# First expert of the second token chunk: where its weight blocks are loaded, summed and split

## The chip, the cores and the metric

One core of a Trainium2 chip. The metric is the device time of one execution in microseconds (us), as the median of the runs. TensorE (PE) multiplies, VectorE (DVE), ScalarE (ACT) and GpSimd (POOL) work beside it, and SyncE (SP) issues nearly all DMA transfers. Each engine works through its own queue in order; semaphores tie the queues together.

## The reference

Rotary attention over 2 batches, 8 heads, 576 positions and head width 64, and then a mixture of four experts on all 1152 tokens of width 512:

```python
out = 0
for e in range(4):
    h = np.maximum(x @ w1[e], 0.0)          # 1152x512 by 512x1024
    out += p[:, e:e + 1] * (h @ w2[e])      # 1152x1024 by 1024x512
```

`x` is the attention output, `p` the normalised domain probabilities. All is float32.

## The kernel before, in words

A float32 operand is held as two float32r parts, high and low, and a product is made of three matmuls (high by high, high by low, low by high). A weight block is 512 KB: two of the eight 128-wide slices of the hidden axis. `Weights.load` brings a block into a raw buffer (`wr`, on SP's queue), and `Weights.split` makes its parts: ScalarE copies the high part (`wh`), and then GpSimd subtracts (`wl`). There are NRAW = 2 raw buffers in the pool `wpool` and a ring of NRING = 5 pairs of split parts. `Weights.next` is one load and one split.

The tokens are done in two chunks: 512 tokens (chunk 0, woven into the attention of the second batch), and then the other 640 (chunk 1, class `Moe1`). In chunk 1 the first layer is done by seven products instead of eight block products: the tokens are cut in two halves of 320, the weight block in four quarters a11, a12, a21, a22, and p1 to p7 are products of sums of token blocks (t1 to t4, class `Quarters`) by quarters or by four sums of quarters (s0 to s3). `Weights.sum` makes those four sums of a block in a buffer `sf` (four instructions of 128x256, line 516), and splits them like a block: `sh` on ScalarE, `sl` on GpSimd. A product is six matmuls of 128x320 (lines 737 to 739). What it leaves in a PSUM bank is worked off by VectorE (adds, line 767, and the low part hL of the hidden values, line 777) and by ScalarE (a copy of p1, line 744, and the high part hH with the relu, line 775). The eight PSUM banks go round: a product takes the bank of the product eight places before it, and waits until that one has been worked off. The second layer (lines 816 to 818) is 120 matmuls of 128x512 for an expert, into five banks `po`; at its end VectorE mixes each bank into `acc` by the probabilities (lines 609 and 611), and the mix of the last expert of a chunk is followed by the DMA of the result (line 617).

Nothing reorders the work here: the order on each engine is that in which the code emits it. Chunk 1's first expert has another order than the rest. Its w1 blocks (key 0) come already split from chunk 0's last steps; then its four w1 blocks are loaded once more for the sums alone (key 2), and then the four w2 blocks (key 1). All p1, then all p2 are done first, and then p6, p7, p5, p4, p3 block by block. In what follows S1 to S4 are the blocks for the sums, W1 to W4 the w2 blocks ("weight blocks 3, 4" of the second layer are W3 and W4), and block 1 to 4 the rounds of the five products. In names as `wr_0_2_1` and `sh_1`, blocks are counted from 0. S3 and S4 have two raw buffers of their own in the pool `sums`, which takes the room that the attention leaves; all other blocks share the two of `wpool`. A load waits until its buffer's last reader is done. The calls of `load`, `split` and `next` between the products in `first_layer` and at the end of the kernel function decide where all this stands.

Of the kernel before, what the change touches and what calls it, by code (L numbers as in the profile page):

```python
# [55 lines left out]
def kernel(  # L56
# [17 lines left out]
    nc = tc.nc  # L74
# [57 lines left out]
    def split(eng_h, eng_l, src, hi, lo):  # L132

        if eng_h is nc.scalar:
            nc.scalar.activation(out=hi, in_=src, func=AF.Copy)  # L135
        elif eng_h is nc.gpsimd:
            nc.gpsimd.tensor_scalar(
                out=hi, in0=src, scalar1=1.0, scalar2=1.0, op0=ALU.mult, op1=ALU.mult
            )
        else:  # L140
            nc.vector.tensor_copy(hi, src)
        eng_l.tensor_tensor(out=lo, in0=src, in1=f32(hi), op=ALU.subtract)  # L142


    class Pair:
# [9 lines left out]
        def load(self, s, queue=nc.sync, heads=((0, 2),)):  # L155

            hp, nm = self.hp, self.nm
            src = {"k": k, "q": q, "v": v}[s]
            x = self.pool.tile([P, 2, NS, D], F32, tag=f"raw{s}", name=f"raw{s}{nm}")
            hs = src[self.b, 2 * hp : 2 * hp + 2]  # L160
            for i, (a, z) in enumerate(heads):
                queue.dma_start(
                    out=x[:, a:z, 0:NR, :], in_=hs[a:z, 0:SM, :].rearrange("h (p r) d -> p h r d", r=NR)
                )
                if i:
                    continue
                for j in range(2):
                    rows = slice(j * ST, (j + 1) * ST)
                    if s == "v":
                        queue.dma_start(out=x[rows, :, NR, :], in_=hs[:, SM:S, :].rearrange("h p d -> p h d"))  # L170
                    else:
                        queue.dma_start(out=x[rows, 0, NR, :], in_=hs[j, SM:S, :])
            self.raw[s] = x
# [285 lines left out]
    class Weights:  # L459
# [14 lines left out]
        def load(self):  # L474
            if self.loaded == len(self.order):
                return
            key = self.order[self.loaded]
            c, e, which, fb = key
            lo, hi = fb * FB * P, (fb + 1) * FB * P
            src, f = (w2[e, lo:hi, :], DM) if which == 1 else (w1[e, :, lo:hi], FB * P)  # L480
            late = which == 2 and fb >= NRAW
            raw = (self.pool if late else wpool).tile(
                [P, FB * DM], F32, tag="raw", name="wr%d_%d_%d_%d" % key, bufs=NRAW
            )
            nc.sync.dma_start(
                out=raw.rearrange("p (a f) -> p a f", f=f), in_=src.rearrange("(a p) f -> p a f", p=P)
            )
            self.raw[key] = raw, f
            self.loaded += 1
# [17 lines left out]
        def sum(self, raw, e, fb):  # L507

            a = raw.rearrange("p (j k h f) -> p j k h f", j=2, h=2, f=P)
            a11, a12, a21, a22 = (a[:, j, :, h, :] for h in range(2) for j in range(2))  # L510
            x = self.pool.tile([P, 4, 2, P], F32, tag="sf", name=f"sf{e}_{fb}", bufs=2)
            for o, p, q, op in (
                (0, a21, a22, ALU.add), (2, a11, a21, ALU.subtract), (1, x[:, 0], a11, ALU.subtract),
                (3, a12, x[:, 1], ALU.subtract),
            ):
                nc.vector.tensor_tensor(out=x[:, o], in0=p, in1=q, op=op)  # L516
            sh, sl = (
                self.pool.tile([P, 4, 2, P], F32R, tag=f"s{t}", name=f"s{t}{e}_{fb}", bufs=NF // FB) for t in "hl"
            )
            split(nc.scalar, nc.gpsimd, x, sh, sl)  # L520
            self.sums[e, fb] = sh, sl
# [177 lines left out]
    class Moe1(Moe):  # L699
# [3 lines left out]
            p1=("a11", "x00"), p2=("a12", "x10"), p3=("s3", "x11"), p4=("a22", "t4"), p5=("s0", "t1"),  # L703
# [78 lines left out]
        def first_layer(self, e):  # L782

            nb = NF // FB
            self.hh = {}
            if e == 0:
                for p in ("p1", "p2"):
                    for i in range(nb):
                        self.product(e, i, p)
                wts.split()  # L790
            for i in range(nb):
                for p in ("p6", "p7", "p5", "p4", "p3") if e == 0 else ("p1", "p6", "p7", "p5", "p2", "p4", "p3"):
                    self.product(e, i, p)
                    if p == "p4" and (e or i):
                        wts.next()
                if e == 0 and i == 0:
                    wts.split()
                elif e == 0 and i in (1, 2):
                    wts.next()
            for f in self.lows:  # L800
                f()
            self.lows = []
# [56 lines left out]
    NE, NRAW, NRING = 3, 2, 5  # L859
    wts = Weights()  # L860
# [201 lines left out]
    with ExitStack() as chunk1:  # L1062
        wts.pool = chunk1.enter_context(tc.tile_pool(name="sums", bufs=1, side="right", reuse_waits="tile"))
        wts.load()
        wts.load()
        wts.split()
        for x in moe0[0].mixes:
            moe0[0].mix(*x)
        chunk0.close()
        wts.load()  # L1070
        wts.split()
        moe = Moe1(chunk1, quarters[0])
        for e in range(E):
            moe.expert(e)
# [43 lines left out]
```

## Time and profile before

| | us |
|---|---|
| median of 3 runs | 579.5 (579.2 to 581.85) |
| span of the profiled execution | 577.8 |
| TensorE busy | 548.1 (95%) |
| VectorE busy | 333.6 (58%) |
| ScalarE busy | 278.9 (48%) |
| GpSimd busy | 334.1 (58%) |

The profile gives the profiled execution's time as its span, from the first to the last instruction; the median of the runs is 1.7 us above that. TensorE is the busiest engine, so the first question is when it stands still, and what ended each of these idle times. The second is at which clock it ran, which the profile gives as the granted share of full speed for any stretch. Attention and chunk 0 end at about 356.7 us from the span's start; first expert, first layer: 356.7 to 384.0; its second layer: 384.0 to 417.4; the other three experts: from 417.4 on.

### The profile page before, as it was taken

To read this page: it belongs to the slowest core of one execution; us is meant where nothing else is said; L and a number is where in the kernel's file an instruction comes from. 1 tells how busy PE (TensorE), PEld (TensorE's weight loads), DVE (VectorE), ACT (ScalarE), POOL (GpSimd) and SP (SyncE) were. 2 spreads that over 40 slices of the span, in tenths; PEclk is the share of its full clock that TensorE was granted. 3 is DMA by queue.
4 is the path that set the end of the run, shared out by engine and by line. 5 is a ranking of instruction groups with operands and counts; after the bars stand their busy time and mean duration, and the time that the engine had idled before them with its cause. 6 is when DMAs were issued, how large, how long until landed. Compare 5 with 4: busy or idle time off the path is not lost.

```text
span 577.8 us, 8600 instructions
## 1 busy us (share of the span) xinstructions
PE 548.1 (95%) x3229; PEld 479.6 (83%) x3229; DVE 333.6 (58%) x590; ACT 278.9 (48%) x545; POOL 334.1 (58%) x228
## 2 busy tenths in 40 slices
PE   4898998999999999999999989879999999999996
PEld 3788877888888888888888878868899899889985
DVE  5588898244363435344245446875777687677702
ACT  5688887555444544554446543453244234324300
POOL 7999964458614972386443493465664674465300
PEclk9999999999999999999999999998999999999999
DMA  5235112252234123422232223423232223223002
GB/s 150 72 112 141 21 45 96 71 175 96 84 100 137 57 71 97 135 75 74 78 97 74 73 67 124 138 74 109 74 110 73 74 79 105 74 73 110 2 0 91
DMA packets 42459, 50.67 MB, mean 88 GB/s; under 512 B 7218, under 2 KB 32050, under 8 KB 42418
## 3 DMA queue, kind: packets, MB, share of 16 engines
q1 hardware_dynamic: 41618, 49.38, 27.9%
q10 hardware_dynamic: 800, 0.75, 0.5%
q8 instruction: 25, 0.41, 0.3%
q14 instruction: 16, 0.13, 0.1%
HBM read 43.34 MB, written 2.36 MB: 79 GB/s over the span
## 4 chain that ended last, share of the span: by engine, by line
PE 74%; DVE 8%; ACT 7%; POOL 5%; issue 2%; DMA 2%; SPq 0%; ACTq 0%; POOLq 0%; DVEq 0%
PE po L816 6%; PE po L817 6%; PE po L818 6%; PE sc L282 5%; PE ph L601 4%; PE ph L603 4%; PE ph L602 4%; PE p L737 4%; PE p L738 4%; PE p L739 4%; PE po L578 4%; PE po L576 4%; PE po L577 4%; PE pp L315 4%; ACT e L301 3%; PE x L417 2%
## 5 line engine op out<-in xcount | busy, mean ns | idle before, releaser
L142 POOL TENSOR_TENSOR wl<-wr,wh 128x1024 fp32r<-128x1024 f32 x64 | 154.9, 2424 | 138.8 <-ACT wh L135 138.8
L135 ACT ACTIVATE wh<-wr 128x1024 fp32r<-128x1024 f32 x64 | 67.4, 1053 | 38.5 <-PE po L578 16.6
L293 DVE TENSOR_REDUCE mx<-sc 128x1 f32<-128x576 f32 x72 | 54.1, 752 | 37.9 <-PE sc L282 37.4
L142 POOL TENSOR_TENSOR sl<-sf,sh 128x1024 fp32r<-128x1024 f32 x16 | 38.4, 2401 | 50.9 <-ACT sh L135 50.9
L816 PE MATMUL po<-wh,hH 128*128 128x512 f32 x160 | 63.6, 398 | 3.1 <-DVE hL L777 3.1
L301 ACT ACTIVATE e<-sc,mx 128x576 f32<-128x576 f32 x72 | 53.3, 740 | 21.8 <-DVE mx L293 21.4
L817 PE MATMUL po<-wl,hH 128*128 128x512 f32 x160 | 63.4, 396 | 0.0
L818 PE MATMUL po<-wh,hL 128*128 128x512 f32 x160 | 63.3, 395 | 0.0
L562 DVE SCALAR_TENSOR_TENSOR hL<-ph,hH 128x512 fp32r<-128x512 f32 x32 | 22.1, 691 | 61.0 <-ACT hH L561 61.0
L576 PE MATMUL po<-wh,hH 128*128 128x512 f32 x128 | 52.3, 409 | 0.0
L601 PE MATMUL ph<-xH,wh 128*128 128x512 f32 x128 | 51.5, 402 | 0.0
L315 PE MATMUL pp<-ident,e 128*128 128x128 f32 x288 | 45.4, 282 | 5.5 <-DVE e L387 3.2
L516 DVE TENSOR_TENSOR sf<-wr 128x256 f32<-128x256 f32 x32 | 40.2, 1294 | 17.8 <-DMA wr<-in_moe_w_dram 17.8
L578 PE MATMUL po<-wh,hL 128*128 128x512 f32 x128 | 50.3, 393 | 0.0
L332 ACT ACTIVATE ptH<-pp 128x512 fp32r<-128x512 f32 x64 | 38.1, 595 | 25.1 <-PE x L365 17.3
L603 PE MATMUL ph<-xH,wl 128*128 128x512 f32 x128 | 50.1, 392 | 0.0
L336 DVE TENSOR_TENSOR ptL<-pp,ptH 128x512 fp32r<-128x512 f32 x64 | 43.9, 685 | 10.8 <-ACT ptH L332 10.3
L602 PE MATMUL ph<-xL,wh 128*128 128x512 f32 x128 | 50.1, 391 | 0.0
L577 PE MATMUL po<-wl,hH 128*128 128x512 f32 x128 | 50.0, 391 | 0.0
L775 ACT ACTIVATE hH<-p 128x320 fp32r<-128x320 f32 x64 | 27.4, 436 | 42.6 <-DVE p L767 42.2
L135 ACT ACTIVATE sh<-sf 128x1024 fp32r<-128x1024 f32 x16 | 17.0, 1061 | 61.9 <-DVE sf L516 61.9
L315 PEld LDWEIGHTS pp<-ident,e 128*128 128x128 f32 x288 | 34.5, 144 | 11.8 <-issue 2.0
(161 smaller groups left out, 1370.0 us busy)
## 6 DMA issues: line engine op xcount, KB each, us to landing
wr<-in_moe_w_dram SPq DMA_DIRECT2D x68, 512.0 KB, 3.5
k2T<-kT SPq DMA_DIRECT2D x14, 288.0 KB, 4.0
rawv<-in_v_dram SPq DMA_DIRECT2D x8, 256.0 KB, 2.9
out_dram<-acc SPq DMA_DIRECT2D x8, 256.0 KB, 2.6
rawk<-in_k_dram SPq DMA_DIRECT2D x7, 256.0 KB, 4.3
rawq<-in_q_dram SPq DMA_DIRECT2D x7, 256.0 KB, 3.0
rawv<-in_v_dram SPq DMA_DIRECT2D x16, 32.0 KB, 2.9
tabs<-in_rope_dram ACTq DMA_DIRECT2D x1, 320.0 KB, 3.5
```

The lines of the kernel that those rows point to most:

```text
L135: nc.scalar.activation(out=hi, in_=src, func=AF.Copy)
L142: eng_l.tensor_tensor(out=lo, in0=src, in1=f32(hi), op=ALU.subtract)
L315: nc.tensor.transpose(pp[:, c * P : (c + 1) * P], self.e[u][:, c * P : (c + 1) * P], ident)
L576: nc.tensor.matmul(po[t], lhsT=sH, rhs=wH, start=(f == 0), stop=False)
L577: nc.tensor.matmul(po[t], lhsT=sH, rhs=wL, start=False, stop=False)
L578: nc.tensor.matmul(po[t], lhsT=sL, rhs=wH, start=False, stop=(f == NF - 1))
L601: nc.tensor.matmul(o, lhsT=wH[:, kt], rhs=xh, start=(kt == 0), stop=False)
L602: nc.tensor.matmul(o, lhsT=wH[:, kt], rhs=xl, start=False, stop=False)
L603: nc.tensor.matmul(o, lhsT=wL[:, kt], rhs=xh, start=False, stop=(kt == KT1 - 1))
L816: nc.tensor.matmul(po[t], lhsT=sH, rhs=wH, start=(f == 0), stop=False)
L817: nc.tensor.matmul(po[t], lhsT=sH, rhs=wL, start=False, stop=False)
L818: nc.tensor.matmul(po[t], lhsT=sL, rhs=wH, start=False, stop=(f == NF - 1))
```

## The change

Four things are changed, all in chunk 1's first expert. W3 and W4 are loaded into the raw buffers of S3 and S4 (`late`). The load of W1 is emitted before chunk 0's last four mixes, the one of W2 after the p1 products, those of W3 and W4 after the p2 products. The four sums of S1 are made on GpSimd instead of VectorE. And the splits stand behind whole rounds of products: S2 between p1 and p2, S3 behind p2, S4 behind block 1, W1 behind block 2, W2 and W3 behind block 3, W4 behind block 4. With that the loads and splits of the following experts stand one call later than before.

```diff
-            late = which == 2 and fb >= NRAW
+            late = c and not e and which and fb >= NRAW
...
-                nc.vector.tensor_tensor(out=x[:, o], in0=p, in1=q, op=op)
+                (nc.vector if e or fb else nc.gpsimd).tensor_tensor(out=x[:, o], in0=p, in1=q, op=op)
...
             if e == 0:
-                for p in ("p1", "p2"):
-                    for i in range(nb):
-                        self.product(e, i, p)
+                for i in range(nb):
+                    self.product(e, i, "p1")
+                wts.next()
+                for i in range(nb):
+                    self.product(e, i, "p2")
+                wts.load()
                 wts.split()
+                wts.load()
             for i in range(nb):
                 for p in ("p6", "p7", "p5", "p4", "p3") if e == 0 else ("p1", "p6", "p7", "p5", "p2", "p4", "p3"):
                     self.product(e, i, p)
-                    if p == "p4" and (e or i):
+                    if p == "p4" and e:
                         wts.next()
-                if e == 0 and i == 0:
+                if e == 0:
                     wts.split()
-                elif e == 0 and i in (1, 2):
-                    wts.next()
+                    if i == 2:
+                        wts.split()
+                    elif i < 2:
+                        wts.load()
...
         wts.load()
         wts.load()
+        wts.load()
         wts.split()
         for x in moe0[0].mixes:
             moe0[0].mix(*x)
         chunk0.close()
-        wts.load()
-        wts.split()
         moe = Moe1(chunk1, quarters[0])
```

SyncE's queue at the end of chunk 0, before (`wr_0_2_n` are S3 and S4, `wr_0_1_n` W1 to W4, `wr_1_0_n` the next expert's first blocks, `acc` the results of chunk 0):

```order
L485 DMA wr_0_2_2_3960<-in_moe_w_dram 128x4x256
L485 DMA wr_0_2_3_3962<-in_moe_w_dram 128x4x256
L617 DMA out_dram<-acc_0_1510 128x512
L617 DMA out_dram<-acc_1_1511 128x512
L617 DMA out_dram<-acc_2_1512 128x512
L617 DMA out_dram<-acc_3_1513 128x512
L485 DMA wr_0_1_0_3983<-in_moe_w_dram 128x2x512
L485 DMA wr_0_1_1_4198<-in_moe_w_dram 128x2x512
L485 DMA wr_0_1_2_4214<-in_moe_w_dram 128x2x512
```

and in the changed kernel:

```order
L485 DMA wr_0_2_2_3960<-in_moe_w_dram 128x4x256
L485 DMA wr_0_2_3_3962<-in_moe_w_dram 128x4x256
L485 DMA wr_0_1_0_3964<-in_moe_w_dram 128x2x512
L617 DMA out_dram<-acc_0_1510 128x512
L617 DMA out_dram<-acc_1_1511 128x512
L617 DMA out_dram<-acc_2_1512 128x512
L617 DMA out_dram<-acc_3_1513 128x512
L485 DMA wr_0_1_1_4036<-in_moe_w_dram 128x2x512
L485 DMA wr_0_1_2_4090<-in_moe_w_dram 128x2x512
```

Only W1's load changes its place in the queue; what W3's and W4's loads wait for is changed by their buffers.

ScalarE's queue at the start of chunk 1, before (`sh_0` and `sh_1` are the high parts of the first two blocks' sums, the four rows of L744 the copies of p1, `hH` the hidden values of p2):

```order
L135 ACTIVATE sh_0_3969<-sf_0_3964 128x1024
L135 ACTIVATE sh_1_3990<-sf_1_3985 128x1024
L744 ACTIVATE p_0_0_4016<-p_0_4009 128x320
L744 ACTIVATE p_0_1_4025<-p_1_4018 128x320
L744 ACTIVATE p_0_2_4034<-p_2_4027 128x320
L744 ACTIVATE p_0_3_4043<-p_3_4036 128x320
L775 ACTIVATE hH_0_0_4051<-p_0_4005 128x320
```

and in the changed kernel:

```order
L135 ACTIVATE sh_0_3971<-sf_0_3966 128x1024
L744 ACTIVATE p_0_0_4007<-p_0_4000 128x320
L744 ACTIVATE p_0_1_4016<-p_1_4009 128x320
L744 ACTIVATE p_0_2_4025<-p_2_4018 128x320
L744 ACTIVATE p_0_3_4034<-p_3_4027 128x320
L135 ACTIVATE sh_1_4043<-sf_1_4038 128x1024
L775 ACTIVATE hH_0_0_4053<-p_0_3996 128x320
```

The second block's sums stand behind the four copies now.

ScalarE's queue from block 3 of the first layer on, before (`wh_0_1_1` to `wh_0_1_3` are W2 to W4; `hH_0_5` and `hH_0_4` belong to block 3, `hH_0_7` to block 4):

```order
L135 ACTIVATE wh_0_1_1_4216<-wr_0_1_1_4198 128x1024
L775 ACTIVATE hH_0_5_4247<-p_2_4239 128x320
L775 ACTIVATE hH_0_5_4247<-p_2_4251 128x320
L135 ACTIVATE wh_0_1_2_4263<-wr_0_1_2_4214 128x1024
L775 ACTIVATE hH_0_4_4072<-p_2_4267 128x320
L135 ACTIVATE wh_0_1_3_4279<-wr_0_1_3_4261 128x1024
L775 ACTIVATE hH_0_7_4310<-p_3_4302 128x320
```

and in the changed kernel:

```order
L135 ACTIVATE wh_0_1_0_4216<-wr_0_1_0_3964 128x1024
L775 ACTIVATE hH_0_5_4249<-p_2_4241 128x320
L775 ACTIVATE hH_0_5_4249<-p_2_4253 128x320
L775 ACTIVATE hH_0_4_4074<-p_2_4263 128x320
L135 ACTIVATE wh_0_1_1_4273<-wr_0_1_1_4036 128x1024
L135 ACTIVATE wh_0_1_2_4277<-wr_0_1_2_4090 128x1024
L775 ACTIVATE hH_0_7_4308<-p_3_4300 128x320
```

W3's high part stood ahead of block 3's last hidden values, and stands behind them now.

## Rows read from the trace of the kernel before

**Rows 1.** Waits, 356 to 420 us: us in total, times, longest us.

```profile
PE po L816 <- DVE hL L777: 3.1, 1, 3.1
PE p L737 <- ACT p L744: 0.9, 1, 0.9
PE p L737 <- DVE acc L611: 0.7, 1, 0.7
PE p L737 <- DVE hL L777: 0.3, 1, 0.3
```

**Rows 2.** Timeline of PE around three waits: start us, us, instruction, [idle before <-releaser].

```profile
360.92 0.31 PE L739 MATMUL p<-xH,wl 128*128 128x320 f32 x1
361.96 0.41 PE L737 MATMUL p<-xH,wh 128*128 128x320 f32 x1 [0.73 <-DVE acc L611]
...
364.55 0.31 PE L739 MATMUL p<-xH,wl 128*128 128x320 f32 x1
365.77 0.42 PE L737 MATMUL p<-tH,sh 128*128 128x320 f32 x1 [0.90 <-ACT p L744]
...
385.19 0.40 PE L818 MATMUL po<-wh,hL 128*128 128x512 f32 x1
388.67 0.79 PE L816 MATMUL po<-wh,hH 128*128 128x512 f32 x1 [3.08 <-DVE hL L777]
```

**Rows 3.** Stretches: length, busy PE PEld DVE ACT POOL, PEclk, DMA share, GB/s.

```profile
384.03:417.42 33.39, 30.31 (x122) 24.50 (x121) 19.85 (x28) 10.09 (x13) 20.38 (x9) 0.90 0.29 94
442.05:469.28 27.23, 27.23 (x122) 22.53 (x121) 20.25 (x27) 9.29 (x12) 16.44 (x7) 1.00 0.24 78
388.67:394.73 6.06, 6.06 (x14) 4.77 (x15) 3.17 (x8) 1.90 (x3) 3.87 (x2) 0.51 0.44 146
```

**Rows 4.** The chain that ended last, 380 to 388 us: start us, us, what.

```profile
380.14 2.41 POOL wl L142
382.57 4.06 DMA wr<-in_moe_w_dram
386.71 1.06 ACT wh L135
```

**Rows 5.** Timeline of DVE at the end of chunk 0.

```profile
354.06 0.49 DVE L644 TENSOR_TENSOR s<-xH,xL 128x320 f32<-128x320 f32 x1
...
357.73 0.75 DVE L516 TENSOR_TENSOR sf<-wr 128x256 f32<-128x256 f32 x2
358.40 0.41 DVE L516 TENSOR_TENSOR sf<-sf,wr 128x256 f32<-128x256 f32 x1
...
359.19 2.72 DVE L611 SCALAR_TENSOR_TENSOR acc<-po,probs,acc 128x512 f32<-128x512 f32 x4
```

**Rows 6.** Timeline of ACT and POOL at the start of chunk 1.

```profile
352.54 0.88 POOL L660 TENSOR_TENSOR t1L<-s,t1H 128x320 fp32r<-128x320 f32 x1
...
365.30 1.40 ACT L744 ACTIVATE p<-p 128x320 f32<-128x320 f32 x4
```

**Rows 7.** Groups by form: line, names, shapes, count | busy us, mean ns | idle before.

```profile
L185 POOL TENSOR_TENSOR t1q<-rawq,tabs 128x256 f32<-128x256 f32 x1 | 0.7, 726 | 0.0
```

**Rows 8.** Timelines of DVE and POOL where both read from SBUF.

```profile
9.66 0.77 DVE L193 TENSOR_TENSOR t1k<-t1k,t2k 128x256 f32<-128x256 f32 x1
...
398.11 3.59 DVE L516 TENSOR_TENSOR sf<-wr 128x256 f32<-128x256 f32 x2
...
398.84 2.59 POOL L142 TENSOR_TENSOR wl<-wr,wh 128x1024 fp32r<-128x1024 f32 x1
```

**Rows 9.** Timeline of DVE in blocks 3 and 4 of the first layer.

```profile
379.94 0.48 DVE L767 TENSOR_TENSOR u<-p,p 128x320 f32<-128x320 f32 x1
...
384.01 0.48 DVE L767 TENSOR_TENSOR u<-p,p 128x320 f32<-128x320 f32 x1
```

**Rows 10.** Timelines of DVE and ACT between the second and third expert.

```profile
466.76 3.47 DVE L611 SCALAR_TENSOR_TENSOR acc<-po,probs,acc 128x512 f32<-128x512 f32 x5 [0.29 <-PE po L818]
...
470.50 0.42 ACT L744 ACTIVATE p<-p 128x320 f32<-128x320 f32 x1
```

## The prediction

> **The bound now.** I read the page's share of busy time first, then the list of waits, then PE's own timeline around each of them, then the granted clock. PE is busy 95% of the span, so only its gaps can be won. From 356 us on the list of waits has four rows for PE [rows 1], all in chunk 1's first expert; the other three experts have none. In PE's timeline three of them are to be seen [rows 2]: a p2 product that waits for the last mix of chunk 0, the first product with sums (p6) that waits for a copy of p1, and the third tile of the second layer, which waits for a low part hL. The 18 matmuls of 320 columns from 361.96 to 364.55 start 0.15 us apart, those of 512 columns 27.23 / 120 = 0.23 [rows 3], so the gaps are 361.96 - 361.07 = 0.89, 365.77 - 364.70 = 1.07 and 388.67 - 385.42 = 3.25 us. The fourth wait is 0.3.
>
> The last gap costs more than its length. The second layer of this expert took 33.39 us, the same 120 matmuls of the next one 27.23 [rows 3]. 3.25 of the 6.16 us between them are the gap; the rest follows it: 14 matmuls from 388.67 to 394.73 ran at a granted clock of 0.51, the lower of the two levels (1.2 instead of 2.4 GHz), in 6.06 us where 14 x 0.227 = 3.18 would do, 2.88 us lost. Behind the gap of 0.89 matmuls still start 0.15 apart, so a gap of that length cost no clock.
>
> The chain of waits says why the third tile waited [rows 4]: GpSimd ended W1's low part at 382.55, only then W3 could be loaded into that raw buffer, the load took 4.06, and ScalarE stood at W3's high part until 386.71 with hidden values of block 3 behind it in its queue. The bank of the third tile was that of block 3's last product, so PE waited for a weight that it didn't need before the layer's fifth step.
>
> **Part 1:** W3 and W4 in buffers of their own, splits behind products. The loads of W3 and W4 now wait for the sums of S3 and S4 on VectorE, not for W1's and W2's splits. By my working below these sums end at about 368.6 and 374.1, against the 382.55 of before; with the 4.06 of the load W3 is there at 373, W4 at 378, and ScalarE takes W3 up behind block 3, after 382. So that DMA wait goes, and with it the gap and the slow clock: 6.16 us [rows 3].
>
> What is late next? The same third tile needs the same hL. Its time is the sum of VectorE's queue from the end of the mixes (361.9, part 3): sums of S2 1.46 (357.73 to 359.19, [rows 5]), the four p2 adds and three of their low parts with one wait for ScalarE, 3.5; sums of S3, held until GpSimd is through with the sums of S2, end 368.6; block 1 in 4.07 (from one block's first add to the next one's, [rows 9]), sums of S4 to 374.1, blocks 2 and 3 to 382.2, and the hL is the second instruction of block 4: done at 383.1. PE starts the second layer 20 products after 364.6. Before, they took 384.03 - 365.77 = 18.26 us [rows 2, 3], about 17.7 without the fourth wait and the restarts; so PE starts at 382.3 and comes to the third tile, six matmuls on, at 383.7. W1's low part, whose split now stands behind block 2, ends at 381.7 by the same count (high part 1.06 behind block 2's last hidden value at 378.3, low part 2.41), and is needed at 382.5. So both are hidden, by 0.6 and 0.8 us; that is thin, and a rival below. If either is late by less than that, nothing; beyond it, the excess is a gap.
>
> **Part 2:** copies of p1 ahead of the sums of S2. Before, ScalarE's four copies (365.30, [rows 6]) stood behind `sh_1`, which waited for VectorE. Now they follow `sh_0` and end near 361. p6 then needs `sl_0`: ScalarE's token parts end by about 358.5 (part 3), `sh` takes 1.06 and `sl` 2.41, the times of `wh` and `wl` of the same shape [rows 4], so 362.0, while PE comes to it at 364.6. The second gap goes: 1.07 us [rows 2]. `sh_1` comes about when its sums are done, and `sl_1` ends at 367, two us before block 2 needs it at 369.
>
> **Part 3:** sums of S1 on GpSimd. This removes 1.46 us from VectorE ahead of the mixes, and adds four instructions to GpSimd. Their price is 0.73 each (the same shape on other tiles, [rows 7]); GpSimd was idle from 353.42, behind its last token part [rows 6], so they lie at 353.5 to 356.8 and hold back nothing on their own engine. But VectorE has its last eight token sums there, from 354.06 [rows 5], with both inputs in SBUF, and these don't run freely beside GpSimd: at 398.11 two sums took 3.59 us instead of 0.75, the second ending at 401.70, just after GpSimd's split of 398.84 ended at 401.43 [rows 5, 8]. Beside short GpSimd instructions one VectorE instruction of 128x256 took 0.77 instead of 0.41 [rows 5, 8]. No row shows these very eight beside the sums, so both sides: at least nothing, at most each sum stops one instruction for all its length, 4 x 0.73 = 2.9. I take the row of short instructions, 4 x 0.36 = 1.4, as its sizes are the nearest. The mixes then start at 357.73 + 1.4 = 359.1, against 359.19 before, take 2.72 [rows 5], and PE's p2 goes on at 361.9 instead of 361.96: 0.1 us, with 0.89 at the one end (the gap goes) and a loss of 1.4 at the other (361.96 to 363.4). W1's load, emitted ahead of the results' DMAs on SP, waits for these sums until about 357, before the mixes are done, so the results aren't held up.
>
> The Trainium skill, page "SBUF — State Buffer", section "Who interferes with whom", says that a VectorE instruction with two SBUF inputs and a GpSimd instruction that reads SBUF can't run together, and that the second one is blocked for the whole of the first. The row at 398.11 agrees, with its 3.59 us. By that rule alone the part would be the loss of 1.4, and the total the first rival's.
>
> **Part 4:** the rest. The fourth wait (0.3, [rows 1]) was for an hL of block 1; by the count above that is done at 375.0 and needed at 375.3, so 0.3 us goes, or nothing. From the second expert on each split stands one call later. The fourth block's sums now follow VectorE's mixes and ScalarE's `sh`, `wh` come ahead of the copy of p1. The mixes end at 470.23, 0.95 us after the third expert starts at 469.28 [rows 3, 10]; 1.46 for the sums and 1.06 each for `sh` and `wh` put the copy's end at 5.0 us after the start instead of 1.6. Its bank is needed by the ninth product, 8 products of six matmuls, 48 x 0.15 = 7.2 us, after the start, so 2 us of cover are left: nothing, three times. Loads of the later blocks still wait for the split two blocks before, as before.
>
> **The sum.** 6.16 + 1.07 + 0.1 + 0.3 = 7.6 us. The profiled execution's span of 577.8 becomes 570.2; the median stands 1.7 above the span, so 579.5 becomes 571.9.
>
> **Rivals.**
> Full blocking of VectorE by the sums: 1.4 lost instead of 0.1 won, all else moves with PE: 573.4. For it speaks the 3.59 us row; against it the 0.77 one. 0.15.
> No blocking: the first gap goes as well, 0.8 more: 571.1. For it: the first of the sums starts 0.6 us before VectorE's first token sum. 0.12.
> A shorter gap in place of the old one: the covers of 0.6 and 0.8 us in part 1 are worked out over twenty us of VectorE queue. If the low part is 2 us later, PE waits 1.4: 573.3. If it is 4 us later the gap is as long as the old one and the clock falls as then, 6.1 back: 578.0. 0.12, mostly the first.
> The change doesn't do what it says, because W2's load behind the results' DMAs holds W3's and W4's back by over 8 us: 578.1 (parts 2 to 4 alone). The loads' causes speak against it: mixes at 361.9, sums of S2 at 363.4. 0.03.
> Slower: the borders between experts. If the copy of p1 comes later than 7.2 us after an expert's start, PE waits at its ninth product, at three borders. With a gap of 3.25 and 2.88 of slow clock at each it is 3 x 6.13 = 18.4: 590.3. It decides from the point where each border costs over 2.5 us. Against it: 2 us of cover and no PE row among the waits there now. 0.04.
>
> **The chances.** The forecast as worked out, 571.9, has 0.54. The bounds of parts 3 and 4 make it 571.1 to 573.7. Below, 0.3 more may come from three slow restarts behind gaps (a first matmul of 0.41 for 0.31, [rows 2]) and 0.3 is the distance from the fastest run to the median: 570.5. Above, a shorter gap may come on top of full blocking, some 1 us: 574.5. The range of 570.5 to 574.5 leaves out the old gap, the change that does nothing, the slower case, and about a tenth of the rest. Half a per cent, 2.9 us, is what a measurement here tells from no change: faster than 576.6 are the forecast, both blocking cases and most of the shorter gaps, 0.91; within it the old gap and the loads, 0.05; slower 0.04.
>
> **To be seen.** Right: no PE wait for hL at the start of the second layer, PEclk 1.00 over its whole length of 27.2 us, p6 directly behind p2, GpSimd's four sums at about 353.5. The price of part 3 is to be read from where the four mixes start: 357.8 if nothing blocks, 359.1 as I take it, 360.6 if all does. Wrong: a DMA row on ScalarE's waits for `wh`, a PE wait at any ninth product of the later experts, or a stretch at half clock anywhere behind 356 us.

## The result and the profile after

The changed kernel takes 573.69 us (median of 4 runs, 572.54 to 574.07) against 579.49 of the kernel before: ratio 0.9892, 95% interval 0.9869 to 0.9915. (A later comparison, that of `e8_after_again` below, has it at 574.79 against 579.09, 0.9925, 0.9899 to 0.9952, which is 0.3 us above the forecast range; all 12 runs of the kernel after have a median of 573.84.) The time of the first comparison lies in the forecast range and the sign is right, but the gain is 5.8 us where 7.6 were forecast. The profiled execution has a span of 571.8 us, 570.2 were forecast.

All lines of this section are of the kernel after. The waits of TensorE from 356 to 420 us (engine, line, releaser: us in total, times, longest us); of the four rows of before [rows 1] one is left:

```profile
PE p L737 <- DVE acc L611: 0.8, 1, 0.8
```

TensorE's timeline around the three places of [rows 2] (lines 822 and 824 were 816 and 818 in the kernel before):

```profile
363.92 0.41 PE L737 MATMUL p<-xH,wh 128*128 128x320 f32 x1 [0.83 <-DVE acc L611]
...
366.51 0.31 PE L739 MATMUL p<-xH,wl 128*128 128x320 f32 x1
366.66 0.31 PE L737 MATMUL p<-tH,sh 128*128 128x320 f32 x1
...
385.41 0.39 PE L824 MATMUL po<-wh,hL 128*128 128x512 f32 x1
385.64 0.39 PE L822 MATMUL po<-wh,hH 128*128 128x512 f32 x1
```

The wait ahead of p2 stays; p6 follows p2 without a gap; the third tile of the second layer (385.64) follows the second 0.23 us later. The second layer and a stretch at 100 us, as stretches (length, busy PE PEld DVE ACT POOL, PEclk, DMA share, GB/s):

```profile
384.25:411.48 27.23, 27.23 (x122) 22.53 (x121) 15.22 (x26) 9.73 (x12) 21.60 (x9) 1.00 0.24 78
100.40:103.80 3.40, 3.40 (x21) 2.91 (x19) 1.16 (x3) 0.38 (x1) 0.00 (x0) 0.51 0.00 0
```

The first answers to [rows 3]: 33.39 us at a granted clock of 0.90 have become 27.23 at 1.00. The second has nothing to do with the change: 255 us ahead of it the clock was at the lower of its two levels for 3.4 us, which the profiled execution of before didn't show.

VectorE at the end of chunk 0, then GpSimd, then ScalarE:

```profile
355.80 0.85 DVE L644 TENSOR_TENSOR s<-xH,xL 128x320 f32<-128x320 f32 x1
356.75 1.79 DVE L649 TENSOR_TENSOR s<-s,s 128x320 f32<-128x320 f32 x2
358.47 1.03 DVE L644 TENSOR_TENSOR s<-xH,xL 128x320 f32<-128x320 f32 x1
359.53 0.49 DVE L649 TENSOR_TENSOR s<-s,s 128x320 f32<-128x320 f32 x1
359.94 1.29 DVE L660 TENSOR_TENSOR tL<-s,tH 128x320 fp32r<-128x320 f32 x3
361.14 2.72 DVE L611 SCALAR_TENSOR_TENSOR acc<-po,probs,acc 128x512 f32<-128x512 f32 x4
```

```profile
355.12 2.13 POOL L516 TENSOR_TENSOR sf<-wr 128x256 f32<-128x256 f32 x2
357.21 0.98 POOL L516 TENSOR_TENSOR sf<-sf,wr 128x256 f32<-128x256 f32 x1
358.27 0.88 POOL L516 TENSOR_TENSOR sf<-wr,sf 128x256 f32<-128x256 f32 x1
361.56 2.38 POOL L142 TENSOR_TENSOR sl<-sf,sh 128x1024 fp32r<-128x1024 f32 x1 [2.41 <-ACT sh L135]
```

```profile
361.38 1.40 ACT L744 ACTIVATE p<-p 128x320 f32<-128x320 f32 x4
...
415.84 0.42 ACT L744 ACTIVATE p<-p 128x320 f32<-128x320 f32 x1
```

Everything here stands later by 358.39 - 356.67 = 1.72 us than in the rows of before, as chunk 1's first product does. The execution falls into three parts at two marks on TensorE: chunk 1's first product, and the first product of the next expert.

| | to the first product | from there to the next expert | from there to the end | span |
|---|---|---|---|---|
| before | 356.67 | 60.75 | 160.4 | 577.8 |
| after | 358.39 | 53.09 | 160.3 | 571.8 |

The middle part, in which all of the change lies, gave 7.66 us, almost the 7.6 of the sum. The first part, whose instructions on TensorE are the same in both kernels, took 1.72 back. If single executions differ by that much in unchanged code, they may also do so in the middle, and an agreement of 0.06 us may be luck. The experiments ask both.

### The profile page after: what moved, and what is told of

Same layout as the page of the kernel before. It is cut to its first block, busy times and chain, and to the rows that moved or that the text cites. A ratio compares the mean times of both kernels' runs of the same rounds, so it can differ in the third digit from the quotient of the medians.

```text
span 571.8 us, 8611 instructions
## 1 busy us (share of the span) xinstructions
PE 545.8 (95%) x3229; PEld 478.5 (84%) x3229; DVE 325.4 (57%) x586; ACT 277.8 (49%) x545; POOL 337.5 (59%) x232
## 4 chain that ended last, share of the span: by engine, by line
PE 78%; DVE 7%; ACT 7%; POOL 4%; issue 2%; DMA 1%; SPq 0%; ACTq 0%; POOLq 0%; DVEq 0%
PE po L824 6%; PE po L822 6%; PE po L823 6%; PE p L737 6%; PE p L739 5%; PE p L738 5%; PE sc L282 5%; PE ph L601 4%; PE ph L603 4%; PE ph L602 4%; PE po L578 4%; PE po L576 4%; PE po L577 4%; PE pp L315 4%; ACT e L301 3%; PE x L417 3%
## 5 line engine op out<-in xcount | busy, mean ns | idle before, releaser
L822 PE MATMUL po<-wh,hH 128*128 128x512 f32 x160 | 62.3, 389 | 0.0
L576 PE MATMUL po<-wh,hH 128*128 128x512 f32 x128 | 52.3, 409 | 0.0
L516 DVE TENSOR_TENSOR sf<-wr 128x256 f32<-128x256 f32 x30 | 32.2, 1114 | 17.4 <-DMA wr<-in_moe_w_dram 17.4
```

Of the source, the lines that this page charges most:

```text
L576: nc.tensor.matmul(po[t], lhsT=sH, rhs=wH, start=(f == 0), stop=False)
L822: nc.tensor.matmul(po[t], lhsT=sH, rhs=wH, start=(f == 0), stop=False)
```

## Experiments

**One execution of each is not enough.** Both kernels were run again, unchanged, for more profiles.

> The kernel before, unchanged, once more. Theory A (the changed stretch gave the 7.7 us that were forecast, and 1.7 us of it were given back some 255 us ahead of it: in the changed kernel TensorE's granted clock fell to 0.50 from 100.4 to 103.8 us, behind the idle time of 1.40 us at 97.0 us, and the kernel before has the same idle time with the clock at 1.00): a fall at 100 us can come in this kernel too, as it hangs on that idle time, which both have. Then this profile shows a granted clock of 1.00 or 0.50 at 100 to 104 us, its span is 577.8 in the one case and 579.5 in the other, and single runs differ by 1.7 us. Theory B (the fall is a result of the change, by another placing of tiles or another start of transfers): never here; clock 1.00 at 100 to 104 us, all spans within 577.5 to 578.1.

> The kernel before, one more profile, to see how much of the two parts of the difference is the single execution. Theory A: the part from the start to chunk 1's first product takes 356.6 to 358.4 us in either kernel, by chance; from there to the end this kernel takes 219.6 to 221.1 us, as the half clock behind the third tile's wait is short or long (2.8 or 6 us, seen so far), with the wait itself at 2.8 to 3.1 us each time. Theory B: both are fixed in the program: 356.7 and 221.1 us again.

> The same once more: theory A, first product at 356.6 to 358.4, from there 219.6 to 221.1 us; theory B, 356.7 and 221.1 us.

> The changed kernel, unchanged, once more, to be compared with the one with the transposes and the mixes first, and to see another of its executions. Theory A (its stretch is fixed, and what differs between executions are falls of the clock elsewhere and small delays of transfers): stretch from the first product to the next expert 53.1 us again, clock falls at another place than 100 us or at the same, spans of single runs from 570 to 574, median time 573.2 to 573.8. Theory B (the fall at 100 us belongs to this program): clock 0.50 at 100 to 104 us again, and all spans 571.5 to 572.3 but the odd one.

> The changed kernel, one more profile. Theory A: first product anywhere from 356.6 to 358.4 us, with or without a fall of the clock at 100 us; from there to the end 213.4 us as in both profiles so far, since no half clock is left in that part. Theory B: first product at 358.4 us and a fall at 100 us again.

> The same once more: theory A, first product at 356.6 to 358.4 us, from there 213.4 us; theory B, first product at 358.4 us with the fall at 100 us.

| | to the first product | to the next expert | to the end | span | low clock at 100 us |
|---|---|---|---|---|---|
| before, as profiled first | 356.67 | 60.75 | 160.4 | 577.8 | no |
| `e1_before_again` | 357.69 | 59.10 | 160.5 | 577.3 | no |
| `e9_before_look1` | 358.27 | 59.16 | 160.4 | 577.8 | yes |
| `e9_before_look2` | 357.25 | 59.29 | 160.4 | 576.9 | no |
| after, as profiled first | 358.39 | 53.09 | 160.3 | 571.8 | yes |
| `e8_after_again` | 357.67 | 53.11 | 160.4 | 571.2 | no |
| `e10_after_look1` | 358.37 | 53.12 | 160.4 | 571.9 | yes |
| `e10_after_look2` | 357.58 | 53.07 | 160.5 | 571.1 | no |

Theory A holds in the main. The low clock at 100 us comes and goes in both kernels, so it isn't of the change. What it costs is read from a short stretch around it, from the transposes behind the idle time at 97 us to a copy on ScalarE; here as first profiled, before and then after:

```profile
98.38 0.63 PE L315 MATMUL pp<-ident,e 128*128 128x128 f32 x4 [1.42 <-DVE e L387]
110.75 1.04 ACT L236 ACTIVATE kT<-tpk 128x1024 fp32r<-128x1024 f32 x1
```

```profile
98.55 0.63 PE L315 MATMUL pp<-ident,e 128*128 128x128 f32 x4 [1.40 <-DVE e L387]
112.36 1.04 ACT L236 ACTIVATE kT<-tpk 128x1024 fp32r<-128x1024 f32 x1
```

That is 110.75 - 98.38 = 12.37 us and 112.36 - 98.55 = 13.81. Over the eight profiles it is 12.29 to 12.37 without the low clock and 13.81 to 13.87 with it, so the low clock costs 1.5 us. The first products of the kernel after differ by less (358.38 against 357.6), since its two executions without the low clock had come to those transposes 0.4 to 0.7 us later than the other two. Two figures of theory A missed: in the kernel before the span was 577.8 with the low clock at 100 us, where 579.5 was expected, and the median of `e8_after_again` is 574.79, where 573.2 to 573.8 was expected. The kernel before compared with itself gave a ratio of 1.0002 (0.9982 to 1.0021). The middle part is fixed in the kernel after, to 0.05 us, and not in the kernel before: three executions of four took 59.1 to 59.3, and the one from which I worked took 60.75. The second layer of three of those four (the first is in [rows 3]), `e1_before_again`, `e9_before_look1`, `e9_before_look2`, columns as above:

```profile
385.08:416.79 31.71, 28.89 (x122) 23.50 (x121) 18.82 (x26) 9.63 (x12) 20.39 (x9) 0.95 0.30 99
```

```profile
385.66:417.43 31.77, 29.14 (x122) 23.59 (x121) 19.03 (x26) 9.58 (x12) 20.37 (x9) 0.95 0.29 97
```

```profile
384.64:416.54 31.90, 29.13 (x123) 23.58 (x122) 19.13 (x26) 9.44 (x12) 20.45 (x9) 0.95 0.29 97
```

The clock over it is 0.95 here and was 0.90 in [rows 3]. TensorE around the third tile in `e9_before_look1` and in `e9_before_look2`:

```profile
386.81 0.40 PE L818 MATMUL po<-wh,hL 128*128 128x512 f32 x1
389.84 0.50 PE L816 MATMUL po<-wh,hH 128*128 128x512 f32 x1 [2.63 <-DVE hL L777]
...
390.64 0.58 PE L816 MATMUL po<-wh,hH 128*128 128x512 f32 x1
...
394.28 0.39 PE L816 MATMUL po<-wh,hH 128*128 128x512 f32 x1
```

```profile
388.97 0.63 PE L816 MATMUL po<-wh,hH 128*128 128x512 f32 x1 [2.77 <-DVE hL L777]
...
392.73 0.40 PE L816 MATMUL po<-wh,hH 128*128 128x512 f32 x1
```

Matmuls take 0.58 to 0.63 us each from 390.64 to about 394 in the one and from 388.97 to 392.4 in the other, while [rows 3] had 0.51 of the clock from 388.67 to 394.73. The gap was 389.84 - 387.04 = 2.80 us in the first, 2.94 in the second and 2.99 in `e1_before_again`; what is left of the excess over 27.23 is the slow clock: 1.74, 1.73 and 1.49 us. In the execution of the prediction it was 3.25 and 2.91. The stretch of low clock was twice as long there: 6.8 us, against 3.4 in the other three. It isn't even in every execution. With one such stretch and no other the mean clock of an execution was 0.996 (`e1_before_again`), with none 0.999 (`e8_after_again`), and 4 of 52 single runs of the kernel before, with 578.4 to 579.7 us, show 0.999.

**W3 and W4 in other buffers, alone.**

```
-            late = which == 2 and fb >= NRAW
+            late = c and not e and which and fb >= NRAW
```

(in the kernel before)

> The kernel before with one part of the change: only the loads of the weight blocks W3 and W4 take the buffers of S3 and S4; order and engines stay as they were. Theory A, by the prediction's first term: the wait of 3.1 us at the third tile of the second layer and the half clock behind it go, 6.1 us together, and the stretch from the first product of the second layer to the next expert takes 27.2 us instead of 33.4; the waits of 0.7 and 0.9 us ahead of p2's first product and of p6 stay. Span 571.7, time 573.4 (1.7 more if the clock falls at 100 us). Theory B for this stretch: the copy of W3 stands in ScalarE's row ahead of the last products' high halves and its GpSimd part behind two others, so that earlier data help little without the new order; then a wait of 1 us or more stays at the third tile, and time is 575 or more.

Time 574.90 us (4 runs), ratio 0.9925 (0.9895 to 0.9955), span 572.8, where theory A had 573.4 and 571.7. The second layer:

```profile
384.60:411.83 27.23, 27.23 (x122) 22.54 (x121) 20.52 (x25) 8.54 (x12) 20.03 (x9) 1.00 0.23 76
```

The third tile's wait and the slow clock are gone, as theory A had it, and the waits ahead of p2 and p6 stay at 0.76 and 0.90. The middle part is 54.63. The third part is 161.0 where it was 160.4, with a new wait of 0.4 us for a low part at 424.7. So the buffers alone are worth 59.2 - 54.6 = 4.6 us, 0.6 of which goes at the next expert.

**The new order without the buffers**, the same line undone in the kernel after:

> The changed kernel with one part undone: W3 and W4 are loaded into the buffers of W1 and W2 again, as before; the new order of loads, sums, splits and products stays. The run before this one (loads alone, old order) took the whole wait at the third tile away. Theory A (either part would do, since the wait needs both a late W3 and W3's copy ahead of the last products' high halves in ScalarE's row): W3 lands 4 us behind the end of W1's low part, at about 386 us on the old kernel's scale, its copy stands behind all first-layer products, its low part is done by 390 us, and TensorE needs it only with the fifth of eight steps, at 397 us; no wait, the stretch from chunk 1's first product to the next expert is 53.1 us, time as the changed kernel's, 573.7. Theory B (the other buffers are needed): the wait comes back at the fifth step or in part at the third tile, the stretch is 54 us or more, time 574.7 or more.

Time 575.52 us, ratio 0.9946 (0.9924 to 0.9967), span 573.1. The middle part is 53.08, as theory A had it: either part takes the third tile's wait away. But the time is not the changed kernel's: the third part took 162.7 instead of 160.4. TensorE at the ninth product of the second expert, which began at 410.38, then ScalarE:

```profile
417.27 0.31 PE L739 MATMUL p<-xH,wl 128*128 128x320 f32 x1
419.11 0.42 PE L737 MATMUL p<-tH,sh 128*128 128x320 f32 x1 [1.53 <-ACT p L744]
```

```profile
416.73 1.06 ACT L135 ACTIVATE sh<-sf 128x1024 fp32r<-128x1024 f32 x1 [5.20 <-DVE sf L516]
417.69 1.04 ACT L135 ACTIVATE wh<-wr 128x1024 fp32r<-128x1024 f32 x1
418.64 0.42 ACT L744 ACTIVATE p<-p 128x320 f32<-128x320 f32 x1
```

This is the place of the slower rival. The copy of p1 ends 419.06 - 410.38 = 8.7 us after the expert's start, 1.5 behind the 7.2 that the rival gave as the point, and the wait is 1.53; one of 0.2 follows at 422.22. Neither theory had it: I looked for the price in the middle part only. The blocks W3 and W4 start the loads of the next expert's blocks; where they end later, the whole row of loads, sums and splits ends later, and the next border pays. Counted from the first product, ScalarE's copy of W4 ends here at 33.7 us, where it was 30.5 in the changed kernel, and its copy of the second expert's last sums at 60.5, where it was 56.6.

**The wait without the slow clock.** In the kernel before, twelve more products on TensorE ahead of the third tile:

```
                 for t in range(n // P):
+                    for _ in range(12 if (e, f, t) == (0, 0, 2) else 0):
+                        nc.tensor.matmul(po[3], lhsT=self.hh[0][0][:, 0:P], rhs=wH, start=True, stop=True)
```

> The kernel before with twelve more products on TensorE ahead of the third tile of the second layer, into the PSUM tile of the fourth (which the fourth's own first product overwrites); the wait itself stays, since nothing that it waits for is moved. It parts the forecast's 6.16 us into the wait and the half clock behind it. Theory A (the clock falls because TensorE has nothing to do in the wait): the twelve take 2.8 us of the wait of 3.1, the clock stays at 1.00 behind it, and the second layer takes 27.2 + 3.1 to 3.3 = 30.3 to 30.5 us instead of 33.4 (31.7 in the second profile of the same kernel); time 576.6. Theory B (the fall does not come from the idle time): the second layer still takes 31.7 us or more, time 579 or more.

```profile
386.97 2.88 PE L816 MATMUL po<-wh,hH 128*128 128x512 f32 x12
389.79 0.50 PE L818 MATMUL po<-wh,hH 128*128 128x512 f32 x1
```

```profile
385.58:415.78 30.20, 30.20 (x134) 24.71 (x133) 17.02 (x25) 9.63 (x12) 19.10 (x9) 1.00 0.32 104
```

(TensorE's timeline, then the second layer.) With TensorE busy through the wait the clock stays at 1.00; the layer takes 30.20 us, so the gap alone is worth 30.20 - 27.23 = 2.97 and the clock behind it 1.5 to 1.7 more, as the further profiles have it. In six of its ten runs the mean clock was 0.999, in the kernel before, in the same comparison, in two of 23. Yet the time is 579.59 us, ratio 1.0008 (0.9987 to 1.0028): nothing gained. From the first product to the end it is 57.58 + 162.1 = 219.7, in `e1_before_again` 59.10 + 160.5 = 219.6. The waits of TensorE behind 405 us, of which the kernel before has none:

```profile
PE p L737 <- DVE hL L777: 0.9, 1, 0.9
PE p L737 <- DVE acc L609: 0.3, 1, 0.3
```

VectorE's last sums for the second expert end as late as before, counted from the first product (mixes begin at 416.84 - 356.67 = 60.2 as first profiled, at 59.8 to 59.9 in the three further profiles, and at 418.12 - 358.20 = 59.9 here), and TensorE, sooner there, waits for what stands behind them. So half of theory A fell: the clock is a matter of the idle wait, but winning it back gained nothing here, where the next expert's blocks didn't start earlier as well, as they do with the change.

**The sums of S1 back on VectorE**, in the kernel after:

```
-                (nc.vector if e or fb else nc.gpsimd).tensor_tensor(out=x[:, o], in0=p, in1=q, op=op)
+                nc.vector.tensor_tensor(out=x[:, o], in0=p, in1=q, op=op)
```

> The changed kernel with one part undone: the four sums of S1 go back to VectorE, behind the token sums and ahead of the mixes; all else stays. This prices the prediction's third term, of which the two traces, 1.72 us apart, give -0.24 us (p2's first product goes on 0.24 us later than before) where +0.1 was forecast. Theory A: on VectorE the four sums take 1.5 us by themselves while the token sums are no longer stretched by GpSimd (1.7 us), so the mixes start 0.2 us earlier, the wait ahead of p2's first product is 0.6 instead of 0.8 us, and the time is within 0.3 us of the changed kernel's: 573.4 to 573.7 (or 571.7 to 572.0 if the clock does not fall at 100 us). Theory B (GpSimd takes the sums off VectorE at little cost): mixes 1.2 us later, wait 2.0 us, p6 later by as much, time 574.9.

Time 573.42 us, ratio 0.9900 (0.9867 to 0.9933), span 570.8. VectorE:

```profile
355.08 1.02 DVE L649 TENSOR_TENSOR s<-s,s 128x320 f32<-128x320 f32 x2
...
358.15 0.75 DVE L516 TENSOR_TENSOR sf<-wr 128x256 f32<-128x256 f32 x2
...
359.62 2.72 DVE L611 SCALAR_TENSOR_TENSOR acc<-po,probs,acc 128x512 f32<-128x512 f32 x4
```

The first product came at 357.10, so the mixes start 2.52 us behind it, as before (359.19 - 356.67 = 2.52), and 2.75 behind it with GpSimd. The sums on GpSimd cost 0.23 us at that place. The middle part is 53.31 against 53.09, since a wait of 0.2 for a low part comes back in block 3: the two cancel, as theory A had it. This edit of the change is worth nothing that the time shows.

**Seven transposes in the idle time at 97 us**, in the kernel after:

```
             pp = banks["pp"].tile([P, 512], F32, f"pp{nm}")
+            for c in range(7 if (self.b, self.hp, u) == (0, NP - 1, TAIL) else 0):
+                nc.tensor.transpose(pp[:, 0:P], ident, ident)
```

> The changed kernel with seven more transposes on TensorE in the idle time at 97 us: the identity, into the part of the PSUM tile that the transposes behind them overwrite; nothing else is moved, and no result uses them. Theory A: with TensorE busy for about 1.1 us of those 1.4 us the granted clock stays at 1.00 from 100 to 104 us, and the 1.7 us come back: span 570.1, time 571.9 to 572.1. Theory B (the fall comes from elsewhere in the changed program and not from the idle time): the clock falls at 100 us all the same, span 571.8, time 573.7. If the transposes delayed the ones behind them, span would be up to 0.3 above theory A's.

The profile has no fall at 100 us and a span of 570.2, theory A's number. But single runs reach from 572.03 to 575.68, median 573.31, ratio 0.9896 (0.9869 to 0.9922), and the kernel after without them has executions without the fall as well. One profile without it shows nothing then; whether the transposes keep it away is open: three of the twelve profiles without them show the fall, and neither of the two with them (the other is that of the next experiment).

**The mixes ahead of the last token parts**, with those transposes. The three low parts of the last quarter (L660) are kept back and emitted behind the four mixes:

```
             for x in moe0[0].mixes:
                 moe0[0].mix(*x)
+            for f in quarters[0].held:
+                f()
```

> The changed kernel with the seven transposes at 97 us, and with the last three token low parts on VectorE put behind chunk 0's four mixes instead of ahead of them. Theory A: the mixes start 1.2 us earlier, the wait of 0.8 us ahead of p2's first product goes, and p6 still follows p2 at once, as the low parts end about where they did (364.0 us on the changed kernel's scale, and p6 is due at 365.8) and the first sums' low part was done at 363.9; stretch from the first product to the next expert 52.3 us instead of 53.1, span 569.4, time 571.2. Theory B: p6 now waits for the moved low parts, or the second block's sums, that stand behind them, come too late (cover about 1 us): stretch 53 us or more, time as with the transposes alone, 573.3.

Time 574.39 us, where the theories had 571.2 and 573.3, against 574.79 of `e8_after_again` in the same comparison; ratio to before 0.9924 (0.9895 to 0.9953) against 0.9925 (0.9899 to 0.9952). The wait ahead of p2 is gone and p6 starts 364.38 - 357.31 = 7.07 us behind the first product instead of 8.27, but the middle part is 53.94, longer by 0.85. VectorE, then GpSimd, then TensorE (this version's lines 518, 613, 662, 743 and 783 are 516, 611, 660, 737 and 777 of the kernel before):

```profile
358.87 2.72 DVE L613 SCALAR_TENSOR_TENSOR acc<-po,probs,acc 128x512 f32<-128x512 f32 x4
361.50 2.54 DVE L662 TENSOR_TENSOR tL<-s,tH 128x320 fp32r<-128x320 f32 x3
363.97 0.74 DVE L518 TENSOR_TENSOR sf<-wr 128x256 f32<-128x256 f32 x2
```

```profile
360.48 2.41 POOL L142 TENSOR_TENSOR sl<-sf,sh 128x1024 fp32r<-128x1024 f32 x1 [2.41 <-ACT sh L135]
```

```profile
371.42 0.42 PE L743 MATMUL p<-t1H,sh 128*128 128x320 f32 x1 [0.48 <-DVE hL L783]
...
376.88 0.42 PE L743 MATMUL p<-t1H,sh 128*128 128x320 f32 x1 [0.79 <-DVE hL L783]
```

Theory B, by another way than it said. In the kernel after, the mixes (one input in PSUM) lie beside GpSimd's split of S1's sums and take the same 2.72 us. Exchanged, the low parts, which read SBUF alone, lie beside it and take 2.54 instead of 1.29, the last ending 1.15 us behind the split. The sums of S2 start 363.97 - 357.31 = 6.66 us behind the first product instead of 5.39, while TensorE is 1.2 us sooner, and it waits for low parts at the third product of blocks 2 and 3. This version doesn't beat the changed kernel.

## Why the prediction came out as it did

**Part 1, the step that was mis-sized.** The mechanism was right: DMA wait, third tile, slow clock, and the new cause of the loads; the second layer takes 27.2 us at clock 1.00 in every profile of the kernel after. The size was that of one execution. Of the 6.16 us, 2.88 were the slow clock as the page of before showed it; in three further executions of the same kernel it was 1.5 to 1.7, and the gap 2.8 to 3.0 instead of 3.25, together 4.48 to 4.67. With those the sum is 7.6 - 1.6 = 6.0, and what was measured is 5.8 in the first comparison and 4.3 in the second, whose interval (2.8 to 5.8 us) ends just short of it. Half of that comparison's six runs of the kernel after took 575.6 to 576.3; no profile shows where, so that stays open. Their mean clocks were 0.991, 0.996 and 0.990, those of the four profiled executions 0.997 to 0.999, so low clock is likely a part of it. The slow clock was the one term that was not made of instructions and waits, and it is the one that didn't repeat. The covers of 0.6 and 0.8 us held: the hL ran at 384.19 to 384.67 against the third tile at 385.64, so 1.0, and W1's low part ended at 383.37 against its first reader at 384.48, so 1.1.

The agreement in the first pair of profiles was luck twice over. The middle part's 7.66 us met the forecast 7.6 because it was measured against the very execution from which I had worked, with its long slow clock. The spans' 6.0 us agree with the corrected sum because that long slow clock (about 1.6 us more than in the others) was set off by the low clock at 100 us (1.5), which of this pair only the kernel after had.

**Part 2** was right: p6 directly behind p2. The copies end at 362.78, 361.06 on the scale of before, where I had them end near 361.

**Part 3** was forecast at +0.1 and came to -0.23, within its ends of +0.89 and -1.4. The stretch of VectorE was 1.69 us (four instructions of 2.0 us in all, by `e4_sums_on_vector`, took 3.67) against the 1.4 that I took; GpSimd's four sums took 4.0 instead of 2.9. The near row, short instructions beside short ones, was the better guide than the 3.59 us row. The Trainium skill's rule (page "SBUF — State Buffer", section "Who interferes with whom"), that of a VectorE instruction with two SBUF inputs and a GpSimd instruction that reads SBUF the second is held for the whole of the first, agrees with `e7_mixes_first`, where the three low parts, 1.29 us by themselves, ended 1.15 us behind GpSimd's split. Short ones nearly took turns: 4.9 us of work of both engines were done in 4.4. The loss of 1.4 us that the prediction drew from the rule did not come, since GpSimd was held as well and VectorE was stretched by 1.69 us and not by 2.9.

**Part 4** was right: the fourth wait went, and all from p6 to the second layer took 384.25 - 366.66 = 17.59 us against 17.7. At the borders the copy of p1 ended 416.26 - 411.48 = 4.8 us after the start, forecast 5.0, and no product waited. Parts 2 to 4 together were forecast at 1.47 and gave 27.36 - 25.86 = 1.50, from the first product to the second layer. That it fits so well is two misses that cancel: up to p2's restart it was -0.24 for the forecast +0.1 (363.92 - 358.39 = 5.53 us against 361.96 - 356.67 = 5.29), and from there on 22.07 - 20.33 = 1.74 for the forecast 1.37. Of the second, 0.26 is that the prediction's own count from 18.26 to 17.7 us gave 0.56, and its sum took only the 0.3 of the wait itself.

**The rivals.** Full blocking, no blocking and a shorter gap did not come. The slower rival's mechanism is real, as `e5_not_late` shows at one border, but the change itself is what keeps it away: with W3 and W4 loaded early the next expert's blocks start early. I had put that effect of the loads nowhere in the sum, and it cost nothing only because both parts of the change came together.

**The part ahead of the change.** The profiled execution of before had the earliest first product of four (356.67), that of after the latest (358.39). Of the 1.72 us between them 1.44 are the low clock at 100 us, by the lines above. The means of four are 357.5 and 358.0, and the ranges overlap; two of the four profiles of the kernel after have the low clock and one of those of before. Less 1.5 us for each of these the means are 357.1 and 357.3. So a difference of the kernels in this part is not shown. The mean of the middle part fell from 59.6 to 53.1, 6.5 us, and the span's from 577.5 to 571.5.

## What to carry to other kernels

A wait has a length that nearly repeats (2.8 to 3.25 us here); a slow clock behind it need not, so take that term from several executions, or give it its own bounds. Ask of every microsecond won on the bounding engine whether the row of loads and splits for the next stage also starts earlier, since otherwise the next border can take it back, as in `e5_not_late` and `e6_busy_wait`. Beside a long GpSimd instruction on SBUF, put VectorE's work that reads one input from PSUM, as the mixes do, and not its work that reads SBUF alone.

## What the runs showed of the hardware

The same program ran with the granted clock at its lower level for 3 to 7 us at places that changed from one execution to the next: from 17 to 24 us in one of the eight profiles of the two kernels, behind the idle time at 97 us in three, and behind the third tile's wait, of different length, in all four profiles of the kernel before. At 100 us it cost 1.5 us each time, behind the third tile's wait 1.5 to 2.9 in the profiles. Keeping TensorE busy through that wait with products that nothing uses kept the clock at 1.00 (`e6_busy_wait`). What decides at 100 us, where TensorE idles alike in both cases (1.40 to 1.42 us in all eight profiles, with and without the fall), stays open.
